# Two more expert weight buffers, one down product, and the kv sums copied by VectorE, in a linear attention and expert kernel

## The chip, the cores and the metric

One core of a Trainium2 chip. The metric is the device time of one execution in microseconds (us). A kernel is timed in several executions, beside executions of the kernel before on the same chip. A ratio is the mean time of one kernel's fast runs over that of the other's of the same rounds, so it isn't quite the ratio of the medians that are quoted (as far as the listed times show, the profiled execution is left out of it). The span of a profile is about 1.7 us shorter than the device time of the same execution.

## The reference, cut to what matters

```python
# S = 2048 tokens, D = 1024, 32 heads of 32, F = 3584, bf16
q, k, v = split(x @ wqkv)
pq, pk = q @ w_phi, k @ w_phi                    # per head
phi = concat(softmax(p), softmax(-p))            # for q and for k
kv, z = phi_k.T @ v, sum(phi_k)                  # per head
a = (phi_q @ kv) / (phi_q @ z) @ wo
# the expert runs for one token only, the one with the largest x @ w_r
y = (silu(x_sel @ w_gate) * (x_sel @ w_up)) @ w_down * sigmoid(r_sel)
out = g * a + (1 - g) * (x, with y added to the row of that token)
```

The expert's weights are 22 MB of the 31 MB that the kernel reads, for a single token. So their loads and their 168 matmuls run beside the attention.

## The kernel before: the parts concerned

TensorE works in three stages: v for all tokens (and w_phi folded into the weights of q and k), then K, then Q. K is a loop of 32 units: eight matmuls into `pk`, two exps on ScalarE, a sum and a reciprocal on VectorE, `phi` on GpSimd (every fourth on VectorE), and five units later eight small matmuls that add phi_k.T @ v into the PSUM tile `kvps`. Q has 32 steps of `pq` (eight matmuls, two exps), `num` (eight matmuls) and `po` (eight, with wo). The program's order is a wish: a scheduler orders each engine's queue when the kernel is built, and each engine then takes its queue in order.

Each expert visit loads chunks of 1 MB into rotating buffers, multiplies, copies the result to `gs` and sends it by four tiny transfers into `gT`, which a "turn" transposes by matmul a few units later.

```python
    GU = (8, 14, 19, 23)          # units with gate and up visits
    TU = (13, 18, 22, 27)         # units with the turns
    DN = 34
    for i in range(NU + LAG):     # NU = 32, LAG = 5
        if i in GU:
            ffn_gu(GU.index(i))
        ...
        if i == DN:
            ffn_down((0, 1, 2, 3), (1, 1, 0, 0))      # the other three chunks: step 11 of Q
        if i >= NU and i - NU < NPRE:
            q_front(0, i - NU)                        # first pq tiles, ahead of Q
        if i >= LAG:
            k_kv(i - LAG)
        if i < NU:
            k_s0(i)
        if i in TU:
            ffn_turn(TU.index(i))
        ...
        if i == 26:
            one_hot_sums()        # a matmul into small_ps, and c8 copied out of it
    kv_finish(range(8), nc.vector.tensor_copy)        # kvps -> KV, 32 x 132 each
    kv_finish(range(8, 16), nc.scalar.copy)
```

`kvps` and `num` share one PSUM buffer.

## Time and profile before

| | before |
|---|---|
| device time, median of 4 | 280.59 us (280.07 to 280.7) |
| span of the profile | 279.5 us |
| TensorE busy | 271.8 us, 97% |
| VectorE, ScalarE, GpSimd busy | 186.2, 121.9, 140.9 us |
| HBM read and written | 31.0 and 4.2 MB |

With one engine at 97%, its holes are what can be won. The lines are shown in the prediction.

### The profile page before, as it was taken

The page shows a single profiled execution, that of the slowest core. Times are in us where ns is not written, and L with a number is a line of the kernel's source. Part 1 is how long each engine was busy: PE and PEld are TensorE (multiplying, and loading weights), DVE is VectorE, ACT ScalarE, POOL GpSimd, SP SyncE. Part 2 cuts the span into 40 slices and gives each one's busy share as a digit, 9 for nine tenths or more (in the row PEclk, how much of TensorE's full clock was granted, in tenths as well). Part 3 has the DMA queues.
Part 4 walks back from the last instruction along what each step waited for, and adds up shares of the span by engine and source line. Part 5 has one row for each costly group of instructions (what it writes and reads, how often), then busy time and mean ns, then how long its engine had stood idle before and what let it go on. Part 6 is the DMA issues. An engine that isn't in the chain of part 4 may idle for free.

```text
span 279.5 us, 5440 instructions
## 1 busy us (share of the span) xinstructions
PE 271.8 (97%) x2022; PEld 149.7 (54%) x2022; DVE 186.2 (67%) x386; ACT 121.9 (44%) x235; POOL 140.9 (50%) x152
## 2 busy tenths in 40 slices
PE   7999999999999999999999899999999999999994
PEld 3666667676544455455554354554555555555442
DVE  3020025566799898699993287888766677899862
ACT  3143332232455546454564657855445543323300
POOL 8000000000087989847862078999566555798310
PEclk9999999999999999999999999999999999999999
DMA  7899993854963788985705817843897244425631
GB/s 257 215 177 187 161 179 76 133 107 130 394 258 114 276 311 298 353 295 189 281 0 188 302 49 260 201 99 13 28 174 202 68 94 125 129 96 133 150 98 62
DMA packets 68767, 47.97 MB, mean 172 GB/s; under 512 B 51376, under 2 KB 56576, under 8 KB 68736
## 3 DMA queue, kind: packets, MB, share of 16 engines
q1 hardware_dynamic: 68240, 47.10, 63.4%
q10 hardware_dynamic: 464, 0.48, 0.5%
q8 instruction: 17, 0.28, 0.4%
q14 instruction: 14, 0.11, 0.1%
q0 software_dynamic: 32, 0.00, 0.0%
HBM read 31.00 MB, written 4.20 MB: 126 GB/s over the span
## 4 chain that ended last, share of the span: by engine, by line
PE 83%; DMA 7%; DVE 4%; issue 2%; ACT 2%; POOL 2%; DVEq 0%; POOLq 0%
PE po L705 20%; PE pq L627 19%; PE pv L536 17%; PE pk L578 11%; PE num L648 6%; DMA wch<-in_B_w_up_dram 3%; DMA mrow<-mi 3%; PE pW L313 2%; PE kvps L602 2%; DVE ssum L586 2%; PE facc L475 1%; PE pv L558 1%; DMA xs_t<-in_A_x_dram 1%; PE kvps L558 1%; PE small_ps L490 1%
## 5 line engine op out<-in xcount | busy, mean ns | idle before, releaser
L578 PE MATMUL pk<-wkf,xT 128*128 128x512 bf16 x256 | 60.4, 379 | 0.0
L627 PE MATMUL pq<-xT,wqf 128*128 128x512 bf16 x256 | 60.2, 379 | 0.0
L677 POOL TENSOR_TENSOR U<-T 128x512 f32<-128x512 f32 x32 | 41.5, 1298 | 34.2 <-DVE T L662 16.7
L705 PE MATMUL po<-wo_sb,oT 128*128 128x512 bf16 (+2 forms) x264 | 58.6, 373 | 0.0
L536 PE MATMUL pv<-wv_sb,xT 128*128 128x256 bf16 (+2 forms) x336 | 52.9, 307 | 0.0
L593 POOL TENSOR_TENSOR phi<-e,rs 128x1024 bf16<-128x1024 bf16 x24 | 45.8, 1912 | 4.0 <-DVE cnd L343 2.4
L586 DVE TENSOR_REDUCE ssum<-e 128x32 f32<-128x1024 bf16 x32 | 38.1, 1194 | 3.8 <-ACT e L582 3.3
L705 PEld LDWEIGHTS <-oT 128*128 128x128 bf16 x264 | 25.4, 98 | 27.8
L536 PEld LDWEIGHTS <-xT 128*128 128x128 bf16 x336 | 31.4, 97 | 14.7
L662 DVE TENSOR_TENSOR T<-num,rq 128x1024 f32<-128x1024 f32 x32 | 38.9, 1215 | 0.0
L543 ACT CAST v_all<-pv 128x384 bf16<-128x384 f32 (+1 forms) x45 | 20.1, 447 | 41.8 <-PE pv L536 36.0
L627 PEld LDWEIGHTS <-wqf 128*128 128x128 bf16 x256 | 23.8, 98 | 24.1 <-issue 0.6
L708 DVE SCALAR_TENSOR_TENSOR o_out<-po,gate,xg 128x512 bf16<-128x512 f32 (+2 forms) x33 | 23.9, 729 | 18.4 <-PE po L705 17.2
L578 PEld LDWEIGHTS <-xT 128*128 128x128 bf16 x256 | 23.0, 97 | 22.8
L678 POOL TENSOR_TENSOR o_sb<-U,rden 128x512 bf16<-128x512 f32 x32 | 33.6, 1049 | 2.5
L581 ACT ACTIVATE e<-pk 128x512 bf16<-128x512 f32 x32 | 19.1, 597 | 32.3 <-PE pk L578 21.9
L629 ACT ACTIVATE E<-pq 128x512 bf16<-128x512 f32 x32 | 19.0, 595 | 30.5 <-PE pq L627 30.2
L423 POOL COPY wch<-wT 1x1 bf16<-1x1 bf16 x3 | 0.4, 177 | 58.6 <-DMA wT<-in_A_wqkv_dram 58.6
L590 POOL TENSOR_TENSOR ksum<-ksum,ssum 128x32 f32<-128x32 f32 x32 | 13.0, 405 | 20.7 <-DVE ssum L586 15.3
L648 PEld LDWEIGHTS <-E 128*128 128x128 bf16 x256 | 16.4, 98 | 10.5 <-DVE T L662 5.2
L648 PE MATMUL num<-KV,E 128*128 128x136 bf16 x256 | 20.7, 223 | 1.0 <-ACT KV L614 1.0
L630 ACT ACTIVATE E<-pq 128x512 bf16<-128x512 f32 x32 | 18.9, 591 | 0.0
(140 smaller groups left out, 253.7 us busy)
## 6 DMA issues: line engine op xcount, KB each, us to landing
wchd<-in_B_w_down_dram SPq DMA_DIRECT2D x7, 1024.0 KB
wch<-in_B_w_up_dram SPq DMA_DIRECT2D x6, 1024.0 KB
wch<-in_B_w_gate_dram SPq DMA_DIRECT2D x4, 1024.0 KB
xin<-in_A_x_dram SPq DMA_DIRECT2D x16, 256.0 KB
out_dram<-o_out SPq DMA_DIRECT2D x30, 128.0 KB
wch<-in_B_w_gate_dram SPq DMA_DIRECT2D x4, 768.0 KB
wv_sb<-in_A_wqkv_dram SPq DMA_DIRECT2D x8, 256.0 KB
wo_sb<-in_A_wo_dram SPq DMA_DIRECT2D x1, 2048.0 KB
```

Source lines behind the costliest of these rows:

```text
L536: nc.tensor.matmul(pv[:, 0:hi - lo], lhsT=xT[:, kb, t * P:(t + 1) * P], rhs=wv_sb[:, kb, lo:hi], start=(kb == 0), stop=(kb == KB - 1))
L543: nc.scalar.copy(out=v_all[:, t, h0:h1, 0:DH], in_=pv[:, 0:(h1 - h0) * DH].rearrange("p (h d) -> p h d", d=DH))
L578: nc.tensor.matmul(pkf, lhsT=xT[:, kb, t * P:(t + 1) * P], rhs=wkf[:, kb, hf * 512:(hf + 1) * 512], start=(kb == 0), stop=(kb == KB - 1))
L586: nc.vector.tensor_reduce(out=ssum[:], in_=e2, axis=AX.X, op=ALU.add)
L593: eng.tensor_tensor(out=phi[:].rearrange("p h s f -> p (h s) f"), in0=e2, in1=_bc(rs[:], [P, HH * 2, DH]), op=ALU.mult)
L627: nc.tensor.matmul(pq[:], lhsT=wqf[:, kb, j * P:(j + 1) * P], rhs=xT[:, kb, sb * SB:(sb + 1) * SB], start=(kb == 0), stop=(kb == KB - 1))
L648: nc.tensor.matmul(num[:, b * NSTR:b * NSTR + KVW], lhsT=E[:, j, sg, tl * P:(tl + 1) * P], rhs=KV[hf][:, sg, jl, :], start=True, stop=True)
L662: nc.vector.tensor_tensor(out=T[:].rearrange("p s (j h) d -> p (s j) h d", h=4), in0=nv[:, :, :, 0:DH], in1=rS.unsqueeze(3).to_broadcast([ ...
L677: nc.gpsimd.tensor_tensor(out=U[:], in0=T[:, 0], in1=T[:, 1], op=ALU.add)
L678: nc.gpsimd.tensor_tensor(out=st["o"][:, hf * HH:(hf + 1) * HH, :], in0=U[:], in1=_bc(rden[:], [P, HH, DH]), op=ALU.mult)
L705: nc.tensor.matmul(po[:, 0:w], lhsT=st["oT"][:, kb, :], rhs=wo_sb[:, kb, sl], start=(kb == 0), stop=(kb == KB - 1))
L708: nc.vector.scalar_tensor_tensor(out=o_out[:, 0:w], in0=po[:, 0:w], scalar=gate[:, t:t + 1], in1=st["xg"][:, sl], op0=ALU.mult, op1=ALU.add)
```

## The change

Its intent is to give the expert's loads more room (wo isn't needed until Q, so its 16 KB of each partition hold two more chunks), to run the expert in four visits (gate; gate and up; the rest of up in one; down in one), to take ScalarE out of the kv copies, and to begin the warm-up matmuls without waiting for a memset. Each letter of a string below names the pool of one chunk: A three buffers, D two, W and V the two in wo's room.

```diff
-    wz = const.tile([P, 512], BF, name="wz")
-    nc.vector.memset(wz[:], 0.0)
...
-            nc.tensor.matmul(small_ps[:, 0:512], lhsT=wz[:, 0:P], rhs=wz[:], start=True, stop=True)
+            nc.tensor.matmul(small_ps[:, 0:512], lhsT=ones, rhs=ones4, start=True, stop=True)
...
-    ones = const.tile([P, P], BF, name="ones")
-    nc.vector.memset(ones[:], 1.0)
+    ones = nc.const_aps.tensor_like(1.0, ident[:])
...
-    wo_sb = big.tile([P, KB, D], BF, name="wo_sb")
...
+    def wbuf(where):
+        if where in "WV":
+            if where == "W":
+                moe["wb"] = wob.tile([P, 2, 4096], BF, name="wch", tag="wo")
+            return moe["wb"][:, "WV".index(where), :]
...
-    spin(6)
+    spin(7)
...
-    GU = (8, 14, 19, 23)
-    TU = (13, 18, 22, 27)
-    DN = 34
+    GU = (8, 14, 21)
+    TU = (13, 18, 26, 27)
+    DN = NU + 3
...
-            ffn_gu(GU.index(i))
+            r = GU.index(i)
+            ffn_gu(r, ("AAAD", "DWVA", "AADD")[r])
+            if r == 2:
+                ffn_gu(3, "WV")
...
-            ffn_down((0, 1, 2, 3), (1, 1, 0, 0))
+            ffn_down(range(7), "AAADDWV")
+            moe_cols()
...
-    kv_finish(range(8, 16), nc.scalar.copy)
+    kv_finish(range(8, 16), nc.vector.tensor_copy)
```

Left out: a second `gs` buffer, a wider `identf` so that the last turn has rows of its own in `gT`, and wo's tile, which is now taken from the pool of W and V at the first num.

More of the change, by code (lines that the diff above doesn't have):

```diff
@@ L183 @@
     w16 = main.enter_context(tc.tile_pool(name="w16", bufs=1))
+    wob = main.enter_context(tc.tile_pool(name="wob", bufs=1))
     ring = main.enter_context(tc.tile_pool(name="ring", bufs=3))
@@ L195 @@
     xs = vscope.enter_context(tc.tile_pool(name="xs", bufs=2))
-    wz = const.tile([P, 512], BF, name="wz")
-    nc.vector.memset(wz[:], 0.0)
     def spin(n):
         for _ in range(n):
-            nc.tensor.matmul(small_ps[:, 0:512], lhsT=wz[:, 0:P], rhs=wz[:], start=True, stop=True)
+            nc.tensor.matmul(small_ps[:, 0:512], lhsT=ones, rhs=ones4, start=True, stop=True)
     ident = const.tile([P, P], BF, name="ident")
     make_identity(nc, ident[:])
-    ones = const.tile([P, P], BF, name="ones")
-    nc.vector.memset(ones[:], 1.0)
+    ones = nc.const_aps.tensor_like(1.0, ident[:])
     BDm = const.tile([P, KB, P], BF, name="BDm")
+    ones4 = nc.const_aps.tensor_like(1.0, BDm[:, 0:4, :].rearrange("p j f -> p (j f)"))
     nc.vector.memset(BDm[:], 0.0)
@@ L228 @@
     hh32 = const.tile([P, NFB, 32], BF, name="hh32")
-    identf = const.tile([P, 16], F32, name="identf")
-    nc.vector.tensor_copy(out=identf[:], in_=ident[:, 0:16])
+    identf = const.tile([P, 32], F32, name="identf")
+    nc.vector.tensor_copy(out=identf[:], in_=ident[:, 0:32])
     gT = const.tile([P, P], F32, name="gT")
@@ L374, in one_hot_cols @@
         er = moe["er"]
-        nc.tensor.matmul(cb_ps, lhsT=ones[:], rhs=hlb[:], start=True, stop=True)
+        nc.tensor.matmul(cb_ps, lhsT=ones, rhs=hlb[:], start=True, stop=True)
         hlc = const.tile([P, 2], F32, name="hlc")
@@ L392, in one_hot_sums @@
         csb = moe["csb"]
-        nc.tensor.matmul(c8_ps, lhsT=ones[:], rhs=csb[:], start=True, stop=True)
+        nc.tensor.matmul(c8_ps, lhsT=ones, rhs=csb[:], start=True, stop=True)
         nc.vector.tensor_copy(out=c8[:], in_=c8_ps[0:KB, :])
@@ L424, in gate_load, with wd_load @@
             fst[len(fst)] = 1
-    def wd_load(c, second):
-        pool, tag = (qp["ring2"], "wch2") if second else (ring, "wch")
-        w = pool.tile([P, 4, D], BF, name="wchd", tag=tag)
-        nc.sync.dma_start(out=w[:], in_=wd_v[:, c * 4:(c + 1) * 4, :])
+    def wbuf(where):
[3 more added lines that the diff above has]
+            return moe["wb"][:, "WV".index(where), :]
+        pool, tag = (qp["ring2"], "wch2") if where == "D" else (ring, "wch")
+        wb = pool.tile([P, 4096], BF, name="wch", tag=tag)
+        return wb[:]
+    def wd_load(c, where):
+        w = wbuf(where).rearrange("p (b n) -> p b n", b=4)
+        nc.sync.dma_start(out=w, in_=wd_v[:, c * 4:(c + 1) * 4, :])
         return w
@@ L433, in ffn_turn @@
         if r < 3:
-            nc.tensor.matmul(ffn_ps[:, 16 * r:16 * r + 16], lhsT=gT[:], rhs=identf[:], start=True, stop=True)
+            nc.tensor.matmul(ffn_ps[:, 16 * r:16 * r + 16], lhsT=gT[:], rhs=identf[:, 0:16], start=True, stop=True)
         else:
             for h in range(2):
-                nc.tensor.matmul(ffn_ps[:, 48:56], lhsT=gT[:], rhs=identf[:, 8 * h:8 * h + 8], start=(h == 0), stop=(h == 1))
+                nc.tensor.matmul(ffn_ps[:, 48:56], lhsT=gT[:], rhs=identf[:, 16 + 8 * h:24 + 8 * h], start=(h == 0), stop=(h == 1))
     def ffn_mid():
@@ L445, in ffn_mid, with gu_load @@
         nc.vector.tensor_tensor(out=hh[:], in0=sg[:], in1=ffn_ps[:, 28:56], op=ALU.mult)
-    def gu_load(r, kp):
+    def gu_load(r, kp, where):
         def part(w, a0, src, k0, nk, col, n):
@@ L451, in part @@
                               in_=src[:, k0:k0 + nk, col * 512:(col + n) * 512])
-        pool, tag = (qp["ring2"], "wch2") if moe["nl"] % 5 >= 3 else (ring, "wch")
-        moe["nl"] += 1
-        w = pool.tile([P, 4096], BF, name="wch", tag=tag)
+        w = wbuf(where)
         gate_load(w[0:1, 0:1])
@@ L466, in gu_load, with ffn_gu @@
         return w
-    def ffn_gu(r):
-        ws = [gu_load(r, k) for k in range(2 if r == 3 else 4)]
+    def ffn_gu(r, bufs):
+        ws = [gu_load(r, k, b) for k, b in enumerate(bufs)]
         acc = psB.tile([P, 512], F32, name="facc", tag="pB")
@@ L478, in ffn_gu @@
                                      tile_position=(0, 32 * g), skip_group_check=True)
-        gs = wk.tile([P, 512], F32, name="gs", tag="junk", bufs=1)
+        gs = wk.tile([P, 512], F32, name="gs", tag="junk", bufs=2)
         nc.scalar.copy(out=gs[:], in_=acc[:])
+        g0 = 16 if r == 3 else 0
         for g in range(4):
-            nc.sync.dma_start(out=gT[4 * g:4 * g + 4, :], in_=gs[32 * g:32 * g + 1, :])
+            nc.sync.dma_start(out=gT[g0 + 4 * g:g0 + 4 * g + 4, :], in_=gs[32 * g:32 * g + 1, :])
     def ffn_down(cs_, pools):
@@ L704, in q_wo @@
             for kb in range(KB):
-                nc.tensor.matmul(po[:, 0:w], lhsT=st["oT"][:, kb, :], rhs=wo_sb[:, kb, sl],
+                nc.tensor.matmul(po[:, 0:w], lhsT=st["oT"][:, kb, :], rhs=moe["wo"][:, kb, sl],
                                  start=(kb == 0), stop=(kb == KB - 1))
@@ L750 @@
     qp["ring2"] = kscope.enter_context(tc.tile_pool(name="ring2", bufs=2))
-    moe["nl"] = 0
     LAG = 5
-    GU = (8, 14, 19, 23)
-    TU = (13, 18, 22, 27)
-    DN = 34
+    GU = (8, 14, 21)
+    TU = (13, 18, 26, 27)
+    DN = NU + 3
     for i in range(NU + LAG):
         if i in GU:
-            ffn_gu(GU.index(i))
+            r = GU.index(i)
+            ffn_gu(r, ("AAAD", "DWVA", "AADD")[r])
+            if r == 2:
+                ffn_gu(3, "WV")
         if i == NU - 1:
@@ L797 @@
         n = i - NL
-        if i == 11:
-            ffn_down((4, 5, 6), (0, 0, 0))
-            moe_cols()
         if i == 24:
@@ L806 @@
             if n == 0:
-                nc.gpsimd.tensor_copy(out=wo_sb[0:1, 0, 0:1], in_=ost[0]["o"][0:1, 0, 0:1])
-                nc.sync.dma_start(out=wo_sb[:], in_=A_wo.rearrange("(kb p) n -> p kb n", p=P))
+                moe["wo"] = wob.tile([P, KB, D], BF, name="wo_sb", tag="wo")
+                nc.gpsimd.tensor_copy(out=moe["wo"][0:1, 0, 0:1], in_=ost[0]["o"][0:1, 0, 0:1])
+                nc.sync.dma_start(out=moe["wo"][:], in_=A_wo.rearrange("(kb p) n -> p kb n", p=P))
             if i == 17:
```

## The prediction

> **What bounds the kernel now.** I read the page's busy totals first, then the 40 slices, then the waits of TensorE, then the timeline around the two places where TensorE really stands.
>
> ```profile
> PE 271.8 (97%) x2022; PEld 149.7 (54%) x2022; DVE 186.2 (67%) x386; ACT 121.9 (44%) x235; POOL 140.9 (50%) x152
> ...
> PE   7999999999999999999999899999999999999994
> ...
> PEclk9999999999999999999999999999999999999999
> DMA  7899993854963788985705817843897244425631
> ...
> PE 83%; DMA 7%; DVE 4%; issue 2%; ACT 2%; POOL 2%; DVEq 0%; POOLq 0%
> ```
>
> The totals say TensorE, 97% of 279.5 us, at full granted clock. A busy TensorE need not be a dense one, because the ends of matmuls are modelled (379 ns for one of 512 columns). So I took start-to-start times: eight matmuls of the q projection fill 1.73 us, 216 ns each, and in the Q phase nine of them and eight of num alternate every 2.46 us (9 x 0.216 + 8 x 0.064) without a hole. So the end is the sum of TensorE's work plus its holes, and only holes can be won. The next view lists TensorE's waits: three between start and end have any size.
>
> ```profile
> PE small_ps L202 <- DVE wz L198: 1.3, 1, 1.3
> PE num L648 <- ACT KV L614: 1.0, 1, 1.0
> PE kvps L602 <- POOL phi L593: 0.5, 1, 0.5
> PE facc L475 <- DMA wch<-in_B_w_up_dram: 0.4, 1, 0.4
> ```
>
> The first is the warm-up, before the first x tile lands. The others are the hand-over from K to Q (1.0), a late phi (0.5) and an expert weight buffer that filled late (0.4). The hand-over in the timeline:
>
> ```profile
> 152.91 2.44 DVE L614 CAST KV<-kvps 32x132 bf16<-32x132 f32 x8 [2.93 <-PE kvps L602]
> ...
> 154.64 0.60 ACT L629 ACTIVATE E<-pq 128x512 bf16<-128x512 f32 x1 [1.15 <-PE pq L627]
> 155.39 2.19 ACT L614 CAST KV<-kvps 32x132 bf16<-32x132 f32 x8 [0.15 <-DVE KV L614]
> ...
> 156.26 0.39 PE L490 MATMUL small_ps<-wchd,hh 128*32 128x512 bf16 x1
> ...
> 157.60 0.60 ACT L630 ACTIVATE E<-pq 128x512 bf16<-128x512 f32 x1
> 157.63 0.57 PE L648 MATMUL num<-KV,E 128*128 128x136 bf16 x7 [0.98 <-ACT KV L614]
> ...
> 158.25 1.89 PE L627 MATMUL pq<-xT,wqf 128*128 128x512 bf16 x8
> ```
>
> VectorE copies eight kv blocks, then ScalarE eight, one after the other and not side by side. ScalarE's eight sit between the two exps of one pq tile (154.64 and 157.60), so that tile's PSUM buffer stays taken and the next pq (158.25) can't start either. TensorE has one 512-column matmul between 156.2 and 157.63.
>
> **What the Trainium skill says.** (1) "TensorE: Matmul & The Clock Gate", Part 3, says that 32-column outputs in distinct column groups run at the same time. The trace agrees: 32 of facc take 1.84 us, 57 ns each, against 216 for a full one. The expert's 168 matmuls are thus 9.7 us of TensorE wherever they stand, and regrouping visits changes nothing in that sum. (2) "PSUM — Partial Sum Buffer", "PSUM bank collisions raise a hardware error": no two engines may touch one bank and quadrant at once, two readers included. The trace agrees in effect: ScalarE's first kv copy starts 0.02 us after VectorE's last ends. So sharing the sixteen copies over two engines never made them parallel. (3) "DMA: Bandwidth & Descriptors", "Queues, rings and completion order": all that SyncE issues runs on one row of rings, and each engine consumes its ring in order. The trace agrees: the 0.1 KB transfer mrow, issued behind three weight loads of 1 MB, took 7.22 us. A small transfer behind big loads is late.
>
> **The change part by part.**
>
> Kv copies by VectorE alone. The eight on ScalarE (264 ns median, 2.19 us) become eight on VectorE (2.44 us for eight, 0.305 each): copies run from 152.91 to 152.91 + 16 x 0.305 = 157.79, 0.2 later than ScalarE's end at 157.58. Alone that costs 0.2. But ScalarE is now free: the second exp follows the first at 155.1 and ends at 155.7 instead of 158.2, so the next pq can run from 156.2, when the two pq in front of it are through, to 157.9. Num starts right behind, its data being ready at 157.8. The hole goes: 157.63 - 156.26 - 0.21 for the single matmul = 1.15 us, and 0.17 us ahead of pq at 158.25 (seven num at 0.064 end at 158.08); about 0.1 may stay. Gain 1.2 us. It assumes that the next pq is ordered ahead of num, as the loop has it.
>
> Two more buffers. The third gate/up visit starts at 112.75; 24 matmuls at 57 ns end at 114.13; its last load came with the wait at 114.65. Hole 0.52 us. Before, that load was issued near 106, behind the tiny gT transfers. With seven buffers, three of the third visit's four loads go into buffers that the first visit gave free at 88; only the last waits for the second visit (101). The visit moves to unit 21: 112.75 + 2 x 1.98 = 116.7. Two microseconds later and an earlier issue: that wait goes. Gain 0.5 us.
>
> Visits merged. The third and fourth visit become one of 1.84 + 0.92 = 2.76 us at 116.7 to 119.5; the down product becomes one of 56 matmuls, 3.2 us, in unit 35, in place of 1.84 there and 1.41 at 168.57. The same matmuls: nothing in the sum, since TensorE is dense at both places. Down's seven loads may start from 119 on.
>
> Wo. It is loaded when the first o tile is ready, as before (issue at 164.92, first use at 190.12, 25 us for 2 MB). Its room is free after the down product near 151. Nothing.
>
> Ones from a constant, wz gone, seven warm-up matmuls for six. TensorE no longer waits to 1.34 for the memset of wz. Cold warm-up matmuls start 0.43 apart; from about 1.0, seven are through by 4.0. The first transposes wait for x at 4.28 in either case. Nothing, at most 0.1 either way. The skill's "TensorE: Matmul & The Clock Gate", Part 1, gives a cold matmul of 512 columns 427 ns; the trace's 0.43 agrees.
>
> VectorE gets 2.44 us more, but at a time when it idles (2.35 busy of 10 us at 150 to 160); a larger identf and a second gs buffer are small.
>
> Sum: 1.2 + 0.5 = 1.7 us of holes gone. The late phi stays: it comes from VectorE's backlog after the routing, which the change leaves. The tail from the last matmul to the end (4 us) stays too.
>
> **The rivals.** First: tiny transfers behind big loads. The results of both merged visits go to gT by eight 2 KB transfers of 0.6 us issue each, from about 119.5; the turns that read them come at the end of units 26 and 27, 119.5 + 6 x 1.98 = 131.4 and 133.4. If four of down's loads are put ahead of them, at 345 GB/s (the rate between 153 and 158) four of 1.05 MB take 12.2 us, and gT lands near 131.5; with six ahead, near 138, and TensorE, which takes its work in order, stands 4 us. For it: before, two down loads were issued between two gT groups, and mrow's 7.22 us. Against: the turns were moved further from the visit than before (three and four units before, five and six now). Time then 279 to 284.
>
> Second: down's loads are late for one single visit. If gT goes first, loads start near 124.5 and all seven need 7 x 3.04 = 21.3 us, to 145.8; unit 35 comes near 148 and wants the last chunk near 151. Slack 2 to 5 us, so probably hidden, and TensorE's 12 us of idle DMA before (138 to 150, at 6 and 13 GB/s) shows that the room is there. If it fails, 1 to 3 us are lost and the time is 280 to 282.
>
> Third: num is ordered before the next pq. Then TensorE stands from 156.2 to 157.8 as before, a bit longer, and only the 0.5 of the weight wait is won: 280.2.
>
> Fourth: a hidden bound takes the gain back later, VectorE, say, whose cycle in the Q phase (reciprocal 0.36, 0.19, T 1.21, plus num 0.65) is also 2.45 us. Against it: 98 matmuls of the output projection run after the last num, so TensorE has work to pull in and the end follows its sum.
>
> **Range and chances.** 280.58 - 1.7 = 278.9; I add 0.2 for the rivals (a tenth of a 2.5 us stall, roughly) and predict 279.1. If all goes well and a bit of the phi wait goes too, 277.9; with a partial stall of the first or second rival, 281.1. Faster by over 2% (under 275.0) asks for 5.6 us, while all holes between start and tail are under 3 us: 1%. Slower by over 2% (over 286.2) asks for a stall above anything that I could construct: 3%. Within 2%: 96%.
>
> **What would show it.** Right: TensorE's list of waits has no entry for num behind KV or for facc behind DMA; at the hand-over pq runs on while VectorE does sixteen copies in 4.9 us; TensorE's busy time falls little (perhaps 271) while the span falls by 1.7. Wrong: an entry of TensorE or its weight loads behind gT (first rival) or behind a down weight (second), or a hole of 1.5 us ahead of the first num behind VectorE's KV (third). If all holes are gone and the time still stands, the fourth holds.

## More of the kernel before

`small_ps` is one PSUM bank that the turns, the one-hot sums, the router and the down product share.

For the comparison later, here are four landmarks of TensorE in the timeline of the kernel before: start, duration, engine, line and operation, output <- inputs, count. They are the first `kvps` of K, the second expert visit, the last `kvps` (two units at once), and the last run of `po`.

```profile
79.86 0.43 PE L602 MATMUL kvps<-v_all,phi 128*128 128x66 bf16 x8
...
100.78 1.91 PE L475 MATMUL facc<-wch,xs 128*32 128x512 bf16 x32
...
152.21 0.67 PE L602 MATMUL kvps<-v_all,phi 128*128 128x66 bf16 x16
...
263.14 12.27 PE L705 MATMUL po<-wo_sb,oT 128*128 128x512 bf16 x64
```

## The result, and the profile after

| | before | after |
|---|---|---|
| device time, median | 280.59 us (280.07 to 280.7) | 278.35 us (278.18 to 278.53) |
| span of the profile | 279.5 us | 276.8 us |
| TensorE busy | 271.8 us | 270.6 us |
| VectorE, ScalarE busy | 186.2, 121.9 us | 189.8, 119.2 us |

The ratio is 0.9924 (95% interval 0.9907 to 0.9941): 2.2 us less, within 2%, where 1.5 had been predicted. TensorE's waits in the changed kernel, from its list (who waited for whom, us in total, times, longest):

```profile
PE small_ps L200 <- PEq L856: 0.9, 1, 0.9
PE small_ps L442 <- DVE c L391: 0.4, 1, 0.4
PE pT L291 <- DVE xT L292: 0.2, 1, 0.2
```

The waits for KV, for phi and for an expert weight are gone. A wait that nobody foresaw has come: the last turn (L442) behind VectorE's copy `c8`. The hand-over from K to Q in the timeline after:

```profile
152.60 5.34 PE L631 MATMUL pq<-xT,wqf 128*128 128x512 bf16 x24
...
152.80 4.89 DVE L618 CAST KV<-kvps 32x132 bf16<-32x132 f32 x16 [3.84 <-PE kvps L606]
...
154.53 0.60 ACT L633 ACTIVATE E<-pq 128x512 bf16<-128x512 f32 x1 [1.15 <-PE pq L631]
155.02 0.59 ACT L634 ACTIVATE E<-pq 128x512 bf16<-128x512 f32 x1
...
157.78 0.64 PE L652 MATMUL num<-KV,E 128*128 128x136 bf16 x8
```

Sixteen copies take 4.89 us on VectorE. The two exps of a pq tile follow each other, the third pq tile runs right behind the second (24 matmuls without a hole), and num starts as the copies end. The same four landmarks as before:

```profile
79.44 0.42 PE L606 MATMUL kvps<-v_all,phi 128*128 128x66 bf16 x8
...
99.46 1.91 PE L478 MATMUL facc<-wch,xs 128*32 128x512 bf16 x32
...
152.09 0.67 PE L606 MATMUL kvps<-v_all,phi 128*128 128x66 bf16 x16
...
259.95 12.27 PE L709 MATMUL po<-wo_sb,oT 128*128 128x512 bf16 x64
```

From these come the lengths of five stretches. The changed kernel does 24 expert matmuls ahead of the last `kvps` that the one before does after it; at the 1.84 / 32 us of a visit they are 1.38 us, which I move back before comparing.

| stretch | before | after | after, with the 1.38 moved back | gain |
|---|---|---|---|---|
| start to first kvps | 79.86 | 79.44 | 79.44 | 0.42 |
| to the second visit | 20.92 | 20.02 | 20.02 | 0.90 |
| to the last kvps | 51.43 | 52.63 | 51.25 | 0.18 |
| to the last run of po | 110.93 | 107.86 | 109.24 | 1.69 |
| to the end of the span | 16.36 | 16.85 | 16.85 | -0.49 |

The sum is the 2.7 us between the two spans. It is 0.5 more than the medians give. The profiled execution of the kernel before took 281.24 us, 0.65 above the median of its timed runs; that of the changed kernel took 278.49. So two single profiles can't be taken for the change. The experiments had to say which of these stretches belong to the change and which to the execution.

### The profile page after: what moved, and what is told of

It is laid out like the page before. It is cut to its first block, busy times and chain, and to the rows that moved or that the text cites. A ratio compares the mean times of both kernels' runs of the same rounds, so it can differ in the third digit from the quotient of the medians.

```text
span 276.8 us, 5433 instructions
## 1 busy us (share of the span) xinstructions
PE 270.6 (98%) x2023; PEld 149.5 (54%) x2023; DVE 189.8 (69%) x392; ACT 119.2 (43%) x227; POOL 141.8 (51%) x152
## 4 chain that ended last, share of the span: by engine, by line
PE 93%; DVE 4%; issue 1%; ACT 0%; DVEq 0%
PE pq L631 20%; PE po L709 20%; PE pv L540 18%; PE pk L582 16%; PE num L652 6%; PE pW L310 3%; PE kvps L606 3%; PE facc L478 2%; DVE ssum L590 2%; PE pv L562 1%; PE kvps L562 1%; PE small_ps L200 1%; PE small_ps L494 1%; DVE hlc L375 1%; PE pT L291 0%
## 5 line engine op out<-in xcount | busy, mean ns | idle before, releaser
L585 ACT ACTIVATE e<-pk 128x512 bf16<-128x512 f32 x32 | 19.1, 597 | 31.0 <-PE pk L582 23.4
L633 ACT ACTIVATE E<-pq 128x512 bf16<-128x512 f32 x32 | 19.0, 595 | 29.2 <-PE pq L631 28.8
L594 POOL TENSOR_TENSOR ksum<-ksum,ssum 128x32 f32<-128x32 f32 x32 | 14.0, 437 | 22.0 <-DVE ssum L590 16.9
L586 ACT ACTIVATE e<-pk 128x512 bf16<-128x512 f32 x32 | 18.9, 591 | 0.0
```

## The experiments

Twelve runs of ten kernels were made, each in five timed rounds beside the kernel before. All were correct. The kernel before has a median of 281.0 to 281.1 us there, 0.5 above the 280.59 of the result, so compare ratios, not medians. One kernel failed in the build: the two buffers together with wz and ones as tiles don't fit. The build says that a pool needs 4 KB of a partition and 2.8 are left. So the constant ones are also what makes room.

### The kv copies alone, twice

```diff
 # on the kernel before
-    kv_finish(range(8, 16), nc.scalar.copy)
+    kv_finish(range(8, 16), nc.vector.tensor_copy)
```

> The kernel before, with the eight kv copies of ScalarE moved to VectorE and nothing else. Theory (the hand-over hole is ScalarE's eight copies sitting between the two exps of one pq tile): the next pq starts near 156.2 in place of 158.25, num has its data after 16 x 0.305 us of copies, the hole of 1.3 us goes, and the time falls by 1.2 to 1.6 us to about 279.2. Rival (num is ordered ahead of the next pq, or VectorE's longer chain takes its place): TensorE still stands 1.5 us ahead of the first num and the time stays within 0.3 us of 280.6.

Measured: 278.75 us, ratio 0.9917 (0.9896 to 0.9937). The stretch from the last kvps to the last run of po is 109.27 us, against 110.93: 1.66 us. The hand-over of this kernel:

```profile
151.94 5.34 PE L627 MATMUL pq<-xT,wqf 128*128 128x512 bf16 x24
...
152.14 4.90 DVE L614 CAST KV<-kvps 32x132 bf16<-32x132 f32 x16 [2.94 <-PE kvps L602]
...
157.12 0.64 PE L648 MATMUL num<-KV,E 128*128 128x136 bf16 x8
```

It is the changed kernel's, from one line. Num itself starts no sooner: 5.69 us after the last kvps, as in the changed kernel, against 5.42 in the kernel before. What is won is that the third pq tile (1.73 us) runs in the time in which num has to wait.

> Once more the kernel before with all sixteen kv copies on VectorE and nothing else. The trace of its first run showed 1.45 us gained at the hand-over; its times showed 2.3, with an interval of 0.6 us either way. Theory: 1.4 to 1.7 us (ratio 0.994 to 0.995). Rival (the copies win something outside the hand-over too): 2.1 to 2.6 us again (0.991 to 0.9925), with the same two traces from the first num on.

Measured: 278.95 us, ratio 0.993 (0.9912 to 0.9948), and 109.28 us for the stretch. The two runs give 2.0 to 2.3 us of time where the traces give 1.66. The interval of the second run reaches down to 1.5 us, which fits; that of the first only to 1.8, just above the traces. What the rest might be comes with the late phi below.

### The kv copies put back on ScalarE in the changed kernel

```diff
 # on the changed kernel
-    kv_finish(range(8, 16), nc.vector.tensor_copy)
+    kv_finish(range(8, 16), nc.scalar.copy)
```

> The changed kernel, with the last eight kv copies back on ScalarE. Theory: the hand-over hole comes back, TensorE stands again about 1 us ahead of the first num and the next pq is late, so the time rises by 1.2 to 1.6 us to about 279.8. Rival (the earlier down product had already removed the hole): same as the changed kernel within 0.3 us.

Measured: 280.13 us, ratio 0.9966 (0.9946 to 0.9987). The hole is back, in TensorE's waits:

```profile
PE num L652 <- ACT KV L618: 1.3, 1, 1.3
```

The stretch is 109.49 us against the changed kernel's 107.86: 1.63 us. The ratio of the changed kernel beside it, in the next call, was 0.9906, so the copies are worth 0.6% or 1.7 us there. Trace and time agree. The earlier down product hadn't removed the hole. No run left eight copies on ScalarE but behind the second exp, so that the parted exps are the cause, and not ScalarE's copies as such, is read from the rows and not tested.

### The start alone, and with the kv copies

```diff
 # on the kernel before: only wz, ones and the count
-    spin(6)
+    spin(7)
```

> The kernel before, with only the constant ones, no wz and seven warm-up matmuls. Theory from the two traces (the warm-up begins at 0.93 in place of 1.34 us, so the clock of TensorE is at full rate when x lands and the transposes run in 60 ns each, not 112): the stage of v begins 0.3 us earlier and the time falls by 0.2 to 0.4 us. Rival (what I predicted: x lands at the same time, nothing): within 0.1 us of the kernel before, and the first transpose at 4.28 with 112 ns each.

Measured: 280.4 us, ratio 0.9976 (0.9952 to 0.9999). The first kvps came at 79.93, no earlier than the 79.86 of the kernel before. In this profile the transposes were slow, in that of the changed kernel fast. The two rows are minimum/median/maximum of the sixteen; first this run, then the changed kernel:

```profile
L291 PE MATMUL pT<-ident,xs_t x16: 219/311/314, 4.2 to 6.6; 128*128 128x128 bf16 x16
```

```profile
L291 PE MATMUL pT<-ident,xs_t x16: 216/218/289, 4.1 to 6.1; 128*128 128x128 bf16 x16
```

The Trainium skill says in "TensorE: Matmul & The Clock Gate", Part 1, that the window which releases the clock is free-running, so that the same kernel can be warm at another point from run to run. This agrees as far as it goes: the changed kernel's second profile, below, has a median of 311 ns again, and its first ten transposes start about 0.11 us apart, where the first eight of the other profile start about 0.07 apart. (The clock column of the profiles reads 1.0 there in both, so that it is the clock is inferred from these lengths.) My theory for this run, a clock that is warm in every execution, fell. In the three profiles with the old start (the kernel before, and two runs of it with only the kv copies changed) the first kvps comes at 79.86, 79.91 and 80.11. In the eleven with the new start it lies between 79.44 and 80.44; the 80.27 among them stands behind a wait for phi, the 80.44 behind a 0.7 us wait for v's weights. A gain of a few tenths may be there; the traces don't show it.

> The kernel before with the kv copies on VectorE, the constant ones and seven warm-up matmuls: the change without its two buffers and its regrouped visits. Theory (the visits win 0.5 us of a weight wait and lose as much to the new wait for c8): the same as the changed kernel within 0.2 us, a ratio near 0.991. Rival (the visits are worth what I predicted, 0.5 us): 0.4 to 0.8 us slower than the changed kernel, 0.993 or more.

Measured: 279.02 us, ratio 0.9958 (0.9922 to 0.9994); two of the six runs were at 281.17 and 281.56, which widens the interval until it overlaps that of the changed kernel. By the medians it is 0.5 us above the changed kernel's second run (278.52), but on another chip. The profiles are firmer: from the second visit to the last run of po this kernel takes 160.88 us, the four profiled changed kernels with all copies and c8 on VectorE take 160.45 to 160.58. So the visits are worth 0.3 to 0.4 us: here the rival was nearer than the theory.

### The changed kernel again

> The changed kernel once more, as the measure for the next three. Expected as measured before: a ratio of 0.992 to 0.993 to the kernel before. If the late phi is a matter of the single execution (it came in the two profiles where the last transposed weight tile, and so the three gate loads, were 1.3 to 1.8 us later), this profile may show it, with mrow landing after 77 us, or not, with mrow before 76.5.

Measured: 278.52 us, ratio 0.9906 (0.9885 to 0.9927). Its profile has the same lengths as the first from the first kvps on: 20.02, 52.63 and 107.82 us. Only the start (80.44) and the tail (16.39, not 16.85) differ. So the tail of +0.49 in my ledger can be of the execution. (A tail above 16.8 us came in five of the nine profiles with the visits and in none of the five without, so that the visits make it likelier isn't excluded.)

The 0.90 us of the second stretch is too. In the twelve profiles whose kernels leave VectorE's order around it alone, the length of the stretch goes with when VectorE could read `mrow`, the router's 0.1 KB transfer that is queued behind three gate loads. These loads wait for the last transposed weight tile. Two rows of the kernel before and, after them, two of the run with only the kv copies changed:

```profile
66.33 1.44 SPq L449 DMA_DIRECT2D wch<-in_B_w_gate_dram  x3
70.08 0.66 SPq L339 DMA_DIRECT2D mrow<-mi  x1
```

```profile
64.88 1.45 SPq L449 DMA_DIRECT2D wch<-in_B_w_gate_dram  x3
70.22 0.66 SPq L339 DMA_DIRECT2D mrow<-mi  x1
```

Where the loads start near 66, mrow is read at 77.3 or later, GpSimd's first phi follow, and a kvps near 94 waits: 20.9 us (two of the twelve). Where they start at 64.4 to 65.6, mrow is read by 76.6, nothing waits, and the stretch is 20.02. I call this the late and the early draw. The run of c8 below, a changed kernel, drew the late case: loads at 66.12, mrow at 77.4, 20.91 us. The kernel before with only another start drew the early one: 64.77, 75.9, 20.02. So both kernels can draw either, and the profile of the kernel before happened to hold the late draw. How often each draws it, the timed runs can't tell, since they have no trace. More late draws in the kernel before would explain why one line of kv copies measured 2.0 to 2.3 us; that stays open.

### The early loads held back

```diff
 # on the changed kernel, in gu_load
+        if r == 1 and where in "WV":
+            for a0 in (0, 1536):
+                nc.gpsimd.tensor_copy(out=w[0:1, a0:a0 + 1], in_=wT[1, KB - 1][0:1, 0, 0:1])
```

> The changed kernel with the two loads into wo's room held back until the last transposed weight tile is there, so that they are issued near 87 and not near 39 us. Theory of the prefetch (the early loads into idle DMA time take 2 MB out of the busy stretch): loads of the second and third visit come later, one facc waits again by about 0.5 us or gT is late, +0.3 to +0.8 us. Rival (two more buffers are enough, whenever they fill): within 0.2 us of the changed kernel.

Measured: 278.55 us, ratio 0.9907 (0.9887 to 0.9927), the stretches 20.02, 52.62 and 107.83. The loads into W and V, which the changed kernel issues at 39 us, came from 79.5 on (not at 87, as expected), and nothing changed. The rival held: that the new buffers fill early has no worth here.

### The down product in two pieces

```diff
 # on the changed kernel
-            ffn_down(range(7), "AAADDWV")
-            moe_cols()
+            ffn_down((0, 1, 2, 3), "DDWV")
...
+        if i == 11:
+            ffn_down((4, 5, 6), "AAA")
+            moe_cols()
```

> The changed kernel with the down product in two pieces as before (four chunks at the end of K, three in the Q phase). Theory (56 matmuls of TensorE cost the same wherever it is dense): within 0.2 us of the changed kernel. Rival (one product saves a change-over or its piece in the Q phase delays the num and VectorE cycle): 0.3 to 0.8 us slower.

Measured: 278.63 us, ratio 0.9913 (0.9892 to 0.9933). The stretches are 51.32 and 109.26, against 52.63 and 107.86 of the changed kernel: 1.31 us less in one, 1.40 more in the other. TensorE is dense in both places, so the piece costs the same in either, to 0.1 us.

### The new wait for c8

TensorE reaches the last turn 0.6 us before it may write. In the changed kernel's timeline:

```profile
130.46 1.89 PE L582 MATMUL pk<-wkf,xT 128*128 128x512 bf16 x8
132.79 0.61 PE L442 MATMUL small_ps<-identf,gT 128*128 128x8 f32 x4 [0.44 <-DVE c L391]
133.26 0.42 PE L606 MATMUL kvps<-v_all,phi 128*128 128x66 bf16 x8
```

Eight pk from 130.46 stream until 132.19 (8 x 0.216); the turn starts at 132.79. `c8` and the turn use different columns of one PSUM bank, and `c8`, 0.13 us long, stands on VectorE behind two sums. The matmul of the one-hot sums, `c8` and the turn in the kernel before, and then the first two in the changed kernel:

```profile
132.30 0.17 PE L393 MATMUL small_ps<-csb,ones 128*128 128x2 bf16 x1
...
133.87 0.14 DVE L394 COPY c<-small_ps 8x2 f32<-8x2 f32 x1
...
134.31 0.51 PE L437 MATMUL small_ps<-identf,gT 128*128 128x8 f32 x4
```

```profile
130.18 0.16 PE L390 MATMUL small_ps<-csb,const-bfloat16-1.0 128*128 128x2 bf16 x1
...
132.60 0.13 DVE L391 COPY c<-small_ps 8x2 f32<-8x2 f32 x1
```

In the five profiles without the visits `c8` starts 1.3 to 1.6 us after that matmul and is done 0.3 to 0.6 us before the turn. In the five with the visits and with `c8` on VectorE it starts 2.4 us after it.

```diff
 # on the changed kernel, in one_hot_sums
-        nc.vector.tensor_copy(out=c8[:], in_=c8_ps[0:KB, :])
+        nc.scalar.copy(out=c8[:], in_=c8_ps[0:KB, :])
```

> The changed kernel, with the tiny copy c8 out of PSUM done by ScalarE in place of VectorE. Theory (the merged visit brings the last turn to the unit after the one-hot sums; its matmul writes the PSUM bank that c8 reads, and c8 sits behind two sums on VectorE, so TensorE stands 0.6 us at 132.2): that wait goes, and the time falls by 0.4 to 0.6 us to about 277.8, below both kernels. Rival (the lost 0.6 us is taken from slack that phi needs anyway): the wait moves to the next kvps and the time stays within 0.15 us of 278.35.

Measured: 278.05 us, ratio 0.9891 (0.9868 to 0.9913), though its profile drew the late phi (that execution took 279.67 us). The wait for c8 is gone from the list, so TensorE did wait for c8. But one step of my theory is wrong: in both programs the sums come in unit 26 and the last turn in unit 27, so the merged visit didn't bring them together. What differs is that VectorE is further behind TensorE there. Two things stand in the timelines: the fourth visit (0.9 us of TensorE from 123.38) no longer comes just before, and VectorE's phi in front of the sums takes 2.1 us, not 1.55. Neither was tested. Nor did a run give c8 a bank of its own, so that it is the bank that orders the two is argued. The run again:

> The changed kernel with c8 copied by ScalarE, once more, as the measure for the next. 0.3 to 0.6 us under the changed kernel (ratio 0.989 to 0.990). The wait for a phi comes in those executions whose mrow lands after 77 us.

Measured: 278.68 us, ratio 0.9919 (0.9899 to 0.9939). Its profile, with an early draw, has 52.31 us from the second visit to the last kvps, against 52.63: half of the 0.6 us is won. Of the other half, 0.2 stands in the list as a new wait:

```profile
PE pq L631 <- ACT e L586: 0.2, 1, 0.2
```

The two ratios average 0.9905, the changed kernel's two 0.9915. A gain of 0.3 us would look like this, but the intervals don't settle it.

### Two tries to take mrow out of the way

```diff
 # on the changed kernel with c8 on ScalarE
-        nc.sync.dma_start(out=mrow[0:1, :, :], in_=mi[:])
+        nc.scalar.dma_start(out=mrow[0:1, :, :], in_=mi[:])
```

> The changed kernel with c8 copied by ScalarE and the 0.1 KB transfer mrow issued from ScalarE's queue, not behind three gate loads on SyncE's. Theory: mrow lands near 72.5 in every execution, VectorE doesn't wait for it, no kvps waits for a phi, and the wait for c8 at 132 is gone: 0.6 us below the changed kernel where its phi was in time and 1.3 where it wasn't, so 277.2 to 277.8. Rival: mrow is as late from the other queue (the 16 engines are full of the gate loads): mrow still near 75 to 77, and only c8's 0.4 to 0.6 us shows; or neither shows and the time stays within 0.2 us of the changed kernel.

Measured: 280.27 us, ratio 0.9969 (0.9948 to 0.999): 1.75 us slower than the changed kernel. Neither theory had this. VectorE's rows around its first read of mrow, in this kernel:

```profile
69.81 2.51 DVE L312 CAST wqf<-pW 128x512 bf16<-128x512 f32 x4
75.07 0.16 DVE L338 TENSOR_REDUCE mxv<-mrow 1x1 f32<-1x16 f32 x1 [2.76 <-DMA mrow<-mi]
75.16 0.67 DVE L312 CAST wqf<-pW 128x512 bf16<-128x512 f32 x1
```

The transfer, issued at 69.82 from ScalarE's queue, was still not there before 75.07. The Trainium skill says in "DMA: Bandwidth & Descriptors", "Issuing engines are not separate DMA queues", that all DMAs run on the same 16 engines and that issuing from several saves only the issuing time. This trace agrees: 5.3 us to the first read, against 5.7 to 6.0 from SyncE's queue in the early draws. But the build now placed the read ahead of two weight copies and a sum that it had followed, and VectorE stood there for 2.76 us. GpSimd's first phi began at 78.31 in place of 76.09, and two kvps waited, at 80.27 and 95.01, 1.1 us in all. The tail is 17.25 us as well, the longest of all; the rest of the loss I can't place.

The opposite, the first read of mrow two sums later (an artificial dependence on the second unit's reciprocal; c8 on ScalarE again):

```diff
+    def route_end():            # the second half of route(), called at unit 1
...
+        nc.vector.tensor_copy(out=mxv[:], in_=moe["rs"][0:1, 0:1])
```

> As the one before, and VectorE's first read of mrow is placed two softmax sums later, so that it doesn't stand in front of them; mrow itself is issued as in the changed kernel. Theory (VectorE's stand of 0.8 to 2.5 us for mrow holds up the sums that GpSimd's first phi need, and so the kvps at 94): no wait for mrow, no kvps behind a phi in any execution, and 0.2 to 0.7 us under the one before, 277.3 to 277.9. Rival (the row of x for the expert now comes too late for the turn at 83.4): TensorE stands there behind the row's transfer by 0.5 us or more, and the time is not below the one before.

Measured: 279.2 us, ratio 0.9934 (0.9916 to 0.9953). VectorE doesn't wait for mrow and no kvps for a phi. But the expert's row of x is now issued at 82.56, and TensorE stands for it:

```profile
84.31 0.18 PE L358 MATMUL small_ps<-ident,rows 128*128 128x8 bf16 x1 [0.64 <-DMA rows<-in_A_x_dram]
```

The rival held. mrow is read early or late, and either end of the chain is tight.

The lengths of the stretches that the argument rests on, from the timelines of all profiles:

| kernel | first kvps to second visit | to last kvps | to last po |
|---|---|---|---|
| before | 20.92 | 51.43 | 110.93 |
| before, start changed | 20.02 | 51.63 | 110.91 |
| before, kv copies (two runs) | 20.03, 20.02 | 51.49, 51.86 | 109.27, 109.28 |
| before, kv copies and start | 20.03 | 51.60 | 109.28 |
| changed, kv copies back | 20.02 | 52.62 | 109.49 |
| changed (two runs) | 20.02, 20.02 | 52.63, 52.63 | 107.86, 107.82 |
| changed, early loads held back | 20.02 | 52.62 | 107.83 |
| changed, down in two | 20.03 | 51.32 | 109.26 |
| changed, c8 on ScalarE (two runs) | 20.91, 20.03 | 52.43, 52.31 | 107.84, 107.86 |
| the same, mrow on ScalarE's queue | 20.92 | 52.42 | 107.84 |
| the same, mrow read later | 20.84 | 52.31 | 107.87 |

## Why the prediction was right, point by point

**The bound.** Right. TensorE was dense apart from its holes, and the gain is holes closed. The two-piece run shows the other half: matmuls moved from one dense place to another cost the same.

**The kv copies, 1.2 us.** The mechanism was right to the row: the exps of one tile are no longer parted, the third pq tile runs at once, num begins at 157.78 (157.9 predicted; the last kvps starts within 0.12 us of the same moment in both profiles) when sixteen copies end after 4.89 us (4.88 predicted). The size was too small: 1.63 to 1.66 us in four pairs of profiles that differ in these copies (to the kernel before, twice; to its new start; to the changed kernel with the copies back). The term that was off is the length of the hole. I took it from 156.26, but 16 pq from 152.72 stream only until 156.18 (0.08); I credited the single expert matmul in it with 0.21 us of useful time, and streamed among others it takes 0.06 (0.15); and the 0.1 us that I let stay didn't stay. That is 0.33 of the 0.43 us. Summed the other way it comes out whole: 1.73 us of pq done ahead of num, less 0.27 for num's later start, plus 0.20 behind it (the 0.17 in front of the next pq, and num no longer in two pieces): 1.66. One reading of the prediction goes too far: that sharing never made the copies parallel because of the PSUM bank. ScalarE waited only 0.15 us for VectorE's last copy; before that it was busy with the first exp of the third tile, behind which its copies stood in its queue.

**The two buffers, 0.5 us.** The weight wait of 0.4 to 0.6 us, which stood in every kernel without the visits, is gone as predicted. Not foreseen was that TensorE, ahead of VectorE by then, comes to the last turn before `c8` has left the same PSUM bank, and 0.6 us go there. The stretch to the last kvps averages 51.60 us in the five profiles without the visits and is 51.32 with the visits and the down product in two: a net of 0.3 us. So the step failed in what it left out, and the total hid it. As waits of 0.5 less 0.6 don't make 0.3, something else helps; fewer change-overs between visits are my guess, not measured. That the loads are issued as early as 39 us counts for nothing.

**Visits merged, and wo: nothing.** Right, to 0.1 us for the down product; wo was in time.

**The start: nothing, 0.1 either way.** Not refuted. The ratio of that run alone points to a small gain, its trace shows none. The start's other worth, room for the two buffers, is in the build.

**The late phi stays.** Right that the change doesn't touch it, but it isn't a fixed part of the kernel: it comes with the execution. The pair of profiles credits the change with 0.9 us for it, wrongly.

**The rivals.** The first (gT behind big loads) and the second (down's loads late) didn't come: the turns waited for no gT and the down product for no weight. The third (num ahead of pq) is refuted by 24 pq in a row. The fourth isn't needed.

Predicted 279.1, measured 278.35: the copies gave 0.4 us more than their term, the visits 0.1 to 0.2 less than theirs, and the 0.2 that I had added for the rivals wasn't needed. The rest of the 0.75 us is within what late draws and intervals leave open. That the total came so near is in part luck: a term too small and a wait not foreseen, of opposite sign.

## What to carry to other kernels

When one engine is dense, list its holes and ask what closes each: here one line of the many carried most of the gain, because it freed an engine that stood between a tile and its release. Where tiny tiles share a PSUM bank and you remove waits of TensorE, look at what of that bank the other engines have still to read when it arrives: the wait can come back there, as 0.6 us did here. And take two profiles of the same kernel before you credit a stretch to a change: 0.9 us here came and went with the execution.

## What the Trainium skill lacked or had wrong

- "PSUM — Partial Sum Buffer", "PSUM bank collisions raise a hardware error": it gives the rule and no sense of its cost in a schedule. A 0.13 us copy of 8 x 2 elements, standing behind two sums on VectorE, held TensorE for 0.6 us in front of a matmul into other columns of the same bank.
- "DMA: Bandwidth & Descriptors", "Queues, rings and completion order": it describes turns between queues by packets, without a figure for how long a tiny transfer waits behind bulk loads. Here 0.1 KB took 5.7 to 7.5 us from issue to first read behind three loads of 1 MB on the same queue and 5.3 us from another queue.
- No page says how far the landing of the same transfers moves from execution to execution. The gate loads, held by a transposed tile, were issued between 64.4 and 66.3 us in the profiles of this case, and 0.9 us of the second stretch went with it.
